# Longer rows for wo and W_down, a last product in rows of 128, and an output stored in eight rows: one change to a cached-attention decode block

## The chip, the cores and the metric

The kernel runs on one core of a Trainium2 chip. The metric is the time of one execution in device microseconds (us). Two times appear below. The time of a run is the metric; the *span* of a profile goes from the first to the last instruction of the profiled execution and is about 1.8 us shorter. Instants such as "659.29" are in us from the start of a profile's span.

## The reference, cut to what matters

Two vectors (B = 2, D = 512) go through one block of attention against a cache and one gated feed-forward block (FFN).

```python
# Hq = Hkv = 32 heads, Sk = 8192, Dh = 128, F = 1376, all bf16
h  = x + (softmax(q @ k.T * Dh**-0.5) @ v).reshape(B, 1, Hq * Dh) @ wo    # q = layernorm(x) @ wq
d  = layernorm(h)
h2 = h + (relu(d @ W_gate) * (d @ W_up)) @ W_down                         # [2, 1, 512]
```

The caches are 268 MB of the 281 MB that have to be read; wo is 4 MB, W_gate, W_up and W_down 1.4 MB each.

## The kernel before: the parts that matter here

SyncE issues all loads on one queue. K and V come in 4 MB tiles (128 partitions of 32 KB) into four slots; a step of the loop takes two heads of one batch, and every second step loads the 256 KB of wo for the four results just made. `O_cur` holds those results with the head dimension on the partitions, so wo is loaded with row `d` of each head on partition `d`: rows of 1 KB.

```python
def load_wo(dst, g, sem):
    nc.sync.dma_start(
        dst[:].rearrange("p (h n) -> p h n", n=D),
        A_wo[2*g*Dh:2*(g+1)*Dh].rearrange("(h d) n -> d h n", d=128)).then_inc(sem, 16)

def collect(T, a):                      # turns the P.V result (rows) into O_cur's layout
    nc.tensor.wait_ge(a2p, a)
    for jj in range(VJ):                # VJ = 4, float32: two passes each
        i = nc.tensor.matmul(Ob[:, 0:4], lhsT=os_sb[:, jj*Dh:(jj+1)*Dh],
                             rhs=sel[:, 4*jj:4*jj+4], start=(jj == 0), stop=(jj == VJ-1))
# ... (the loop: scores, exp, P.V, collect, o_proj with wo_cur) ...
```

At the end W_up, W_gate and W_down are loaded into a free slot. `slot[0]` holds, per partition, four rows of W_up and of W_gate, and W_down in 1 KB rows (row `r*128 + p` on partition `p`):

```python
for k, (r0, r1) in enumerate(WD_PARTS):                       # ((0, 6), (6, 10))
    nc.sync.dma_start(slot[0][:, 2*DC*F + r0*D:2*DC*F + r1*D].rearrange("p (r n) -> p r n", n=D),
        B_W_down[r0*128:r1*128].rearrange("(r p) n -> p r n", p=128)).then_inc(sem_wd[k], 16)
# ...
def ffn_in(dst, w, f0, f1):                                   # W_up, then W_gate
    for f in range(f0, f1):
        fw = 128 if f < 10 else FR                            # FR = 96, DC = 4
        for c in range(DC):
            i = nc.tensor.matmul(dst[0:fw, f*B:(f+1)*B],
                lhsT=w[:, c, f*128:f*128 + fw],               # weights: contiguous columns
                rhs=d_b[:, c*B:(c+1)*B], start=(c == 0), stop=(c == DC-1))
    return pe.run(i)
# ... hd = relu(gate) * up, in two halves ...
for k, (f0, f1) in enumerate(((0, FH), (FH, FC))):            # FH = 6, FC = 11
    pe.wait(t_hd[k], (sem_wd[k], 16))
    for f in range(f0, f1):
        for c in range(DC):                                   # result: 128 partitions x 8
            i = nc.tensor.matmul(Op[0][:, c*B:(c+1)*B], lhsT=wdn[:, f, c, :], # (wd_last for f = 10)
                                 rhs=hd[0:kp, f*B:(f+1)*B], ...)
# ... two VectorE operations add h ...
nc.sync.dma_start(out[:, 0].rearrange("b (p c) -> p b c", c=DC),              # 256 pieces of 8 bytes
                  o_c[:].rearrange("p (b c) -> p b c", b=B)).then_inc(sem_out, 16)
```

The softmax here doesn't subtract the row's maximum and nothing guards it: scores larger than these inputs give would overflow.

Of the kernel before, what the change touches and what calls it, by code (L numbers as in the profile page):

```python
# [7 lines left out]
F32 = mybir.dt.float32  # L8
BF16 = mybir.dt.bfloat16
# [30 lines left out]
def bass_sequential_preLN__gqa_block_cached__glu_gated_reglu__decode_kernel(  # L40
# [16 lines left out]
    DC = D // 128  # L57
# [13 lines left out]
    WD_PARTS = ((0, 6), (6, 10))  # L71

    with ExitStack() as es:
# [19 lines left out]
        sem_wd = [S(f"wd{i}") for i in range(3)]  # L93
# [28 lines left out]
        zr = sb("zr", [128, 4], F32)  # L122
        zi = sb("zi", [128, 4], F32)
        O_cur = sb("O_cur", [128, 4], BF16)
# [4 lines left out]
        r2 = sb("r2", [128, B], F32)  # L129
# [3 lines left out]
        o_c = sb("o_c", [128, B * DC], BF16)  # L133
# [18 lines left out]
        with nc.Block() as block:  # L152

            @block.sync
            def _(eng):
# [4 lines left out]
                def load_wo(dst, g, sem):  # L160
                    nc.sync.dma_start(
                        dst[:].rearrange("p (h n) -> p h n", n=D),
                        A_wo[2 * g * Dh:2 * (g + 1) * Dh].rearrange("(h d) n -> d h n", d=128)).then_inc(sem, 16)
# [7 lines left out]
                nc.sync.dma_start(wd_last[:], B_W_down[F - FR:]).then_inc(sem_wd[2], 16)  # L171
# [10 lines left out]
                for c in range(4):  # L182
                    pool.last()
                    pool.run(nc.gpsimd.tensor_copy(
                        out=sel[32 * c:32 * c + 32, :].rearrange("p (j q a) -> p j q a", j=VJ, q=PG),
                        in_=ident_f[32 * c:32 * c + 32, 32 * c:32 * c + 16].rearrange("p (q j a) -> p j q a", j=VJ, q=PG)))
# [163 lines left out]
                def collect(T, a):  # L350
                    nc.tensor.wait_ge(a2p, a)
                    for jj in range(VJ):
                        i = nc.tensor.matmul(  # L353
                            Ob[:, 0:4], lhsT=os_sb[:, jj * Dh:(jj + 1) * Dh],
                            rhs=sel[:, 4 * jj:4 * jj + 4], start=(jj == 0), stop=(jj == VJ - 1))
                    T.mark("ob", i)

                def z_sum(T, bank):
                    T.mark("z", nc.tensor.matmul(  # L359
                        bank[:, ZC:ZC + 8], lhsT=ones_f[:], rhs=zs[:], start=True, stop=True))  # L360

                def o_proj(T, w, b0, b1, last=False):
                    wv = w[:].rearrange("p (h n c) -> p h c n", n=128, c=DC)
                    for h in range(2):
                        for c in range(DC):
                            i = nc.tensor.matmul(
                                Wp[:, c * B + b0:c * B + b1], lhsT=wv[:, h, c, :],
                                rhs=O_cur[:].rearrange("p (b a) -> p a b", a=2)[:, h, b0:b1],
# [3 lines left out]
                with nc.Fori(0, NI, engines=OrderedEngineSet([nc.tensor.engine])):  # L372
# [7 lines left out]
                    o_proj(body, wo_cur, 0, B)  # L380
# [18 lines left out]
                o_proj(tail, wo_cur, 0, B)  # L399
# [30 lines left out]
                def normalize(bank, t_z):  # L430
                    dve.wait(t_z)
                    dve.run(nc.vector.tensor_reduce(  # L432
                        out=zr[:], in_=bank[:, ZC:ZC + 8].rearrange("p (n k) -> p n k", k=2), axis=AX.X, op=ALU.add))
# [4 lines left out]
                def o_scale(t_ob):  # L438
                    dve.wait(t_ob)
                    nc.vector.tensor_tensor(out=O_cur[:], in0=Ob[:, 0:4], in1=zi[:], op=ALU.mult).then_inc(d2p, 1)  # L440

                t_dm, t_s = {}, {}
                for p in range(NP):
# [76 lines left out]
                    elif p == NP - 2:  # L520
# [5 lines left out]
                        for k, (r0, r1) in enumerate(WD_PARTS):  # L526
                            nc.sync.dma_start(  # L527
                                slot[0][:, 2 * DC * F + r0 * D:2 * DC * F + r1 * D].rearrange("p (r n) -> p r n", n=D),
                                B_W_down[r0 * 128:r1 * 128].rearrange("(r p) n -> p r n", p=128)).then_inc(sem_wd[k], 16)
# [10 lines left out]
                o_proj(tail, wo_last, 0, B, last=True)  # L540
# [18 lines left out]
                wdn = slot[0][:, 2 * DC * F:2 * DC * F + 10 * D].rearrange("p (r n c) -> p r c n", c=DC, n=128)  # L559
                wdl = wd_last[:].rearrange("p (n c) -> p c n", c=DC)  # L560
                pe.wait(t_d)

                def ffn_in(dst, w, f0, f1):
                    for f in range(f0, f1):
                        fw = 128 if f < 10 else FR
                        for c in range(DC):
                            i = nc.tensor.matmul(
                                dst[0:fw, f * B:(f + 1) * B], lhsT=w[:, c, f * 128:f * 128 + fw],
# [3 lines left out]
                FH = 6  # L572
                pe.wait((sem_w[0], 16))
                t_u = ffn_in(Sp[1], wup, 0, FC)
                pe.wait((sem_w[1], 16))
                t_g = (ffn_in(Op[1], wgt, 0, FH), ffn_in(Wp, wgt, FH, FC))

# [79 lines left out]
```

## Time and profile before

| | before |
|---|---|
| time, median of the first three runs | 665.84 us (665.70 to 665.99) |
| bytes read, mean rate over the span | 281.05 MB, 423 GB/s |
| busy: DVE, TensorE | 70%, 51% |
| last load (W_down's second part) lands | 659.29 us |
| output issued, landed | 660.72, 663.63 us |

The first lines are from the profile's page: the span; the share of time in which the 16 DMA engines were busy, in 40 slices (tenths, 9 is 90% or more); their packets by size; and the engines' shares of the chain of waits that ended last.

```profile
span 664.0 us, 7589 instructions
...
DMA  9999999999999999999999999999999999999996
...
DMA packets 15856, 281.20 MB, mean 423 GB/s; under 512 B 1666, under 2 KB 7140, under 8 KB 7140
...
DMA 71%; DVE 26%; PE 1%; ACT 0%; issue 0%; SPq 0%; DVEq 0%
```

No slice but the last is below nine tenths. The DMA engines never rest until the last weights are in, so each nanosecond that a packet costs is a sixteenth of a nanosecond of the kernel's time. DVE's 26% of the chain is no contradiction: VectorE frees the slots, but each load is issued about 28 us before it lands.

Grouped by size, the packets' records in the trace give what a packet costs (not a view of the profile but worked out from its packet records): 8192 of 32768 B at a mean of 1220.8 ns, 256 of 11008 B at 417.0 ns, and 5474 of 1024 B at 47.8 ns.

```
packet size    before: count, mean ns     after: count, mean ns
32768 B        8192   1220.8              8192   1219.8
11008 B         256    417.0               256    418.1
 5120 B           -                        128    199.1
 4096 B           -                        128    161.9
 2048 B           -                       2048     85.2
 1024 B        5474     47.8               226     46.1
```

A line through the first two is about 10 ns per packet plus 37.8 ns per KB, and the small ones lie on it.

Next is the tail, from the timeline before. A line gives the start and the duration in us, the engine, the line of the program, the operation, what it writes and reads, how many, and in brackets how long the engine had been idle before it and what ended that.

```profile
650.93 1.06 PE L353 MATMUL Ob<-sel,os_sb 128*128 128x4 f32 x8 [0.70 <-ACT os_sb L535]
...
653.51 1.25 PEld L567 LDWEIGHTS S<-d_b,slot 128*128 128x128 bf16 x44 [0.34 <-DVE d_b L552]
...
655.96 0.72 PEld L567 LDWEIGHTS O<-d_b,slot 128*128 128x128 bf16 x24 [1.21 <-DMA slot<-in_B_W_gate_dram]
655.97 0.80 PE L567 MATMUL O<-d_b,slot 128*128 128x2 bf16 x24 [1.12 <-DMA slot<-in_B_W_gate_dram]
656.61 0.82 PEld L567 LDWEIGHTS W<-d_b,slot 128*128 128x128 bf16 x20
...
658.16 0.93 PE L611 MATMUL O<-hd,slot 128*128 128x2 bf16 x24 [0.59 <-DMA slot<-in_B_W_down_dram]
659.42 0.67 PE L611 MATMUL O<-hd,slot 128*128 128x2 bf16 x16 [0.33 <-DMA slot<-in_B_W_down_dram]
...
660.34 0.35 DVE L618 SCALAR_TENSOR_TENSOR o_c<-O,r,hb 128x4 bf16<-128x4 f32 x2 [2.35 <-PE O L611]
660.72 0.39 SPq L623 DMA_DIRECT2D out_dram<-o_c  x1
```

TensorE collects the last results (L353), multiplies W_up (the first L567), then waits 1.12 us for W_gate and 0.59 and 0.33 us for the two parts of W_down (L611). So here, too, the loads set the pace; TensorE's reserve is about 2 us in all.

### The profile page before, as it was taken

What the parts mean: (1) busy time and instruction counts of PE and PEld (TensorE: products, weight loads), DVE (VectorE), ACT (ScalarE), POOL (GpSimd) and SP (SyncE); (2) the same over time, 40 slices, a digit from 0 to 9 for tenths busy, and PEclk for the clock granted to TensorE, in tenths of its full rate; (3) what the DMA queues carried; (4) which work ended last, traced back from release to release, by engine and by line L of the source; (5) the groups of instructions that cost most, each with busy time, mean ns of one, the idle gap of its engine ahead of it and who ended that gap; (6) DMA issues with size and microseconds to landing.
All of it is one profiled execution on the core that took longest, in us unless ns stands there. A gap on an engine that the chain in (4) does not pass through costs nothing.

```text
span 664.0 us, 7589 instructions
## 1 busy us (share of the span) xinstructions
PE 339.3 (51%) x3223; PEld 220.8 (33%) x3223; DVE 465.7 (70%) x275; ACT 198.5 (30%) x416; POOL 194.1 (29%) x48
## 2 busy tenths in 40 slices
PE   2535554446545445643536545445653535554665
PEld 2413332324333223432314333222432323342444
DVE  1756887767688676787767688676678767678671
ACT  0603332223332123332213332123333213333360
POOL 2022333332233331233332133332133332134000
PEclk9999566555555665566556655665555556555657
DMA  9999999999999999999999999999999999999996
GB/s 379 413 440 424 433 438 427 430 424 428 436 438 426 420 426 438 427 435 425 430 430 428 436 418 442 423 426 436 427 434 430 428 432 426 434 427 434 428 417 239
DMA packets 15856, 281.20 MB, mean 423 GB/s; under 512 B 1666, under 2 KB 7140, under 8 KB 7140
## 3 DMA queue, kind: packets, MB, share of 16 engines
q1 hardware_dynamic: 15840, 281.06, 99.2%
q8 instruction: 5, 0.08, 0.0%
q14 instruction: 7, 0.06, 0.0%
q10 hardware_dynamic: 4, 0.00, 0.0%
HBM read 281.05 MB, written 0.00 MB: 423 GB/s over the span
## 4 chain that ended last, share of the span: by engine, by line
DMA 71%; DVE 26%; PE 1%; ACT 0%; issue 0%; SPq 0%; DVEq 0%
DMA slot<-in_A_k_cache_dram 64%; DVE prod L466 16%; DVE tb L474 7%; DMA slot<-in_B_W_down_dram 5%; DVE prod L474 3%; DMA slot<-in_A_wq_dram 2%; PE W L229 1%; ACT q_b L276 0%; PE O L271 0%; DVE q L249 0%; PE O L611 0%; SPq L523 0%; SPq L527 0%; DVE tb L262 0%; PE S L240 0%
## 5 line engine op out<-in xcount | busy, mean ns | idle before, releaser
L455 POOL COPY q2c<-q 128x8 bf16<-128x8 bf16 x32 | 190.3, 5947 | 417.2 <-DMA slot<-in_A_k_cache_dram 359.6
L466 DVE TENSOR_TENSOR prod<-slot,q_b 128x12288 bf16<-128x12288 bf16 (+1 forms) x32 | 207.7, 6492 | 130.4 <-DMA slot<-in_A_k_cache_dram 128.8
L325 PE MATMUL T<-ident_f,slot 128*128 128x128 f32 x528 | 136.5, 426 | 219.3 <-POOL q2c L455 217.0
L491 ACT ACTIVATE kT<-T 128x1024 bf16<-128x1024 bf16 x132 | 131.6, 1022 | 390.4 <-PE T L325 386.2
L325 PEld LDWEIGHTS T<-ident_f,slot 128*128 128x128 f32 x528 | 98.2, 218 | 233.4 <-POOL q2c L455 230.8
L474 DVE TENSOR_TENSOR tb<-prod 128x6144 bf16<-128x6144 bf16 (+1 forms) x64 | 136.8, 2137 | 2.2
L343 PE MATMUL O<-slot,e 128*32 128x512 bf16 x1024 | 114.7, 613 | 18.5 <-ACT e L423 18.5
L474 DVE TENSOR_TENSOR prod<-tb 128x3072 bf16<-128x3072 bf16 (+1 forms) x64 | 73.4, 1148 | 2.2
L313 PE MATMUL S<-q2c,kT 128*128 128x4 bf16 x1056 | 50.4, 170 | 37.7 <-ACT kT L491 37.7
L313 PEld LDWEIGHTS S<-q2c,kT 128*128 128x128 bf16 x1056 | 44.1, 108 | 67.8 <-ACT kT L491 65.9
L343 PEld LDWEIGHTS O<-slot,e 128*32 128x32 bf16 x1024 | 31.9, 132 | 76.2 <-issue 53.4
L353 PE MATMUL Ob<-sel,os_sb 128*128 128x4 f32 x136 | 31.0, 351 | 26.3 <-ACT os_sb L499 25.6
L353 PEld LDWEIGHTS Ob<-sel,os_sb 128*128 128x128 f32 x136 | 29.5, 320 | 28.1 <-ACT os_sb L499 26.9
L479 DVE TENSOR_REDUCE scores<-prod 128x96 f32<-128x768 bf16 (+1 forms) x32 | 30.2, 945 | 1.1
L423 ACT ACTIVATE e<-scores 64x96 bf16<-64x96 f32 (+1 forms) x64 | 19.6, 307 | 22.8 <-DVE scores L479 22.0
L432 DVE TENSOR_REDUCE zr<-Ob 128x4 f32<-128x8 f32 x15 | 2.5, 166 | 28.1 <-PE Ob L353 28.1
L423 ACT ACTIVATE e<-S 64x32 bf16<-64x32 f32 (+1 forms) x64 | 13.1, 204 | 14.9 <-PE S L313 14.5
L423 ACT ACTIVATION_READ_ACCUMULATOR e<-S 64x1 f32 x64 | 12.9, 201 | 0.7
L423 ACT ACTIVATION_READ_ACCUMULATOR e<-scores 64x1 f32 x64 | 11.8, 185 | 0.0
L359 PEld LDWEIGHTS Ob<-zs,ones_f 128*128 128x128 f32 x30 | 6.5, 269 | 11.6 <-issue 11.6
L499 ACT ACTIVATE os_sb<-O 128x512 f32<-128x512 f32 x16 | 9.6, 597 | 0.4
L276 ACT ACTIVATE q_b<-O 128x512 bf16<-128x512 f32 x8 | 4.3, 595 | 17.0 <-PE O L271 17.0
(74 smaller groups left out, 70.4 us busy)
## 6 DMA issues: line engine op xcount, KB each, us to landing
slot<-in_A_k_cache_dram SPq DMA_DIRECT2D x32, 4096.0 KB, 28.1
slot<-in_A_v_cache_dram SPq DMA_DIRECT2D x31, 4096.0 KB, 31.6
slot<-in_A_wq_dram SPq DMA_DIRECT2D x1, 4096.0 KB, 12.3
slot<-in_A_v_cache_dram SPq DMA_DIRECT2D x2, 2048.0 KB, 29.5
wo_cur<-in_A_wo_dram SPq DMA_DIRECT2D x15, 256.0 KB, 27.1
slot<-in_B_W_up_dram SPq DMA_DIRECT2D x1, 1376.0 KB, 26.7
slot<-in_B_W_gate_dram SPq DMA_DIRECT2D x1, 1376.0 KB, 29.8
slot<-in_B_W_down_dram SPq DMA_DIRECT2D x1, 768.0 KB, 31.4
```

Of the source, the lines that this page charges most:

```text
L229: i = nc.tensor.matmul(Wp[:, h * B:(h + 1) * B], lhsT=wq[:, c, h * Dh:(h + 1) * Dh], rhs=lT[:, c * B:(c + 1) * B], start=(c == 0), stop=(c ...
L313: i = nc.tensor.matmul(Sp[p % 2][:, 2 * jj:2 * jj + 4], lhsT=kv_[:, k, r, :], rhs=q2c[p % 2][:, r, :], start=(r == 0), stop=(r == 1))
L325: i = nc.tensor.transpose(Tp[g % 2][:, k * 128:(k + 1) * 128], k_t[:, j:j + 2, :].rearrange("p j d -> p (j d)").bitcast(F32), ident_f[:])
L343: i = nc.tensor.matmul(Op[0][c:c + 32, :], lhsT=e_t[q][:, j // VJ, :], rhs=v_t[:, j:j + VJ, :].rearrange("p j d -> p (j d)"), start=(q == ...
L353: i = nc.tensor.matmul(Ob[:, 0:4], lhsT=os_sb[:, jj * Dh:(jj + 1) * Dh], rhs=sel[:, 4 * jj:4 * jj + 4], start=(jj == 0), stop=(jj == VJ - 1))
L423: i = nc.scalar.activation(out=e_t[q][h, j0 // VJ:j1 // VJ, 8 * q:8 * q + 8].rearrange("p g (j a) -> p g j a", a=2)[:, :, :, a], in_=src(h ...
L455: nc.gpsimd.tensor_copy(out=q2c[p % 2][:], in_=q2[:, p]).then_inc(g2p, 1)
L466: t_dm[p] = dve.run(nc.vector.tensor_tensor(out=prod[:, 0:jd, :], in0=k_t[:, 0:jd, :], in1=qv, op=ALU.mult))
L474: dve.run(nc.vector.tensor_tensor(out=o, in0=cur[:, :, 0:half], in1=cur[:, :, half:w], op=ALU.add))
L479: t_s[p] = dve.run(nc.vector.tensor_reduce(out=sc[:, 0:jd], in_=cur, axis=AX.X, op=ALU.add))
L491: to_pe(nc.scalar.activation(out=kT[gg % 2][:], in_=Tp[gg % 2][:].bitcast(BF16), func=ACT.Copy))
L499: to_pe(nc.scalar.activation(out=os_sb[:], in_=Op[0][:], func=ACT.Copy))
```

## The change

Its intent is to make the packets fewer and the end shorter. wo comes in 2 KB rows (two rows of wo per partition), so O has to be taken out with `2*p + r` as its index: the collect becomes 16 products of 64 columns. W_down comes in rows of 5, 4 and 1 KB (ten rows per partition), so the index of `hd` on partition `p` is `10*p + f`, and W_up and W_gate are read as weights with a step of 10 columns. The last product has `hd` as the weights and W_down as the moving operand, its result lies in rows of 128, h is transposed to match, and two DMAs store four rows of 256 B each.

```diff
-    WD_PARTS = ((0, 6), (6, 10))
+    WD_PARTS = ((0, 5), (5, 9), (9, 10))
 ... load_wo
-                        dst[:].rearrange("p (h n) -> p h n", n=D),
-                        A_wo[2 * g * Dh:2 * (g + 1) * Dh].rearrange("(h d) n -> d h n", d=128)).then_inc(sem, 16)
+                        dst[:], A_wo[2 * g * Dh:2 * (g + 1) * Dh].rearrange("(p r) n -> p (r n)", r=2)).then_inc(sem, 16)
 ... collect
-                    for jj in range(VJ):
-                        i = nc.tensor.matmul(
-                            Ob[:, 0:4], lhsT=os_sb[:, jj * Dh:(jj + 1) * Dh], ...
+                    for r in range(2):
+                        for jj in range(VJ):
+                            for a_ in range(2):
+                                i = nc.tensor.matmul(
+                                    Ob[64 * a_:64 * a_ + 64, B * r:B * r + B],
+                                    lhsT=os_sb[:].rearrange("p (j d r) -> p j r d", j=VJ, r=2)[:, jj, r, :], ...
 ... W_down
-                                B_W_down[r0 * 128:r1 * 128].rearrange("(r p) n -> p r n", p=128)).then_inc(sem_wd[k], 16)
+                                B_W_down[0:10 * 128].rearrange("(p r) n -> p r n", r=10)[:, r0:r1]).then_inc(sem_wd[k], 16)
 ... ffn_in
-                                dst[0:fw, f * B:(f + 1) * B], lhsT=w[:, c, f * 128:f * 128 + fw],
+                                dst[0:fw, f * B:(f + 1) * B],
+                                lhsT=w[:, c, f:10 * 128:10] if f < 10 else w[:, c, 10 * 128:],
 ... between W_up and W_gate: h into rows
+                for k in range(4):
+                    for c in range(DC):
+                        i = nc.tensor.matmul(
+                            Tp[0][32 * k:32 * k + B, c:128:DC], lhsT=hb[:, c * B:(c + 1) * B],
+                            rhs=ident[:, 32 * k:32 * k + 32], start=True, stop=True)
 ... the last product (hd is now made in one piece)
+                    for m in range(4):
+                        i = nc.tensor.matmul(
+                            Op[0][32 * m:32 * m + B, 0:128], lhsT=hd[0:kp, f * B:(f + 1) * B],
+                            rhs=(wdn[:, f, :] if f < 10 else wd_last[:])[:, 128 * m:128 * m + 128], ...
 ... the store
-                nc.sync.dma_start(
-                    out[:, 0].rearrange("b (p c) -> p b c", c=DC),
-                    o_c[:].rearrange("p (b c) -> p b c", b=B)).then_inc(sem_out, 16)
+                for b, e in enumerate((nc.sync, nc.scalar)):
+                    e.dma_start(
+                        out[b, 0].rearrange("(k n) -> k n", n=128), o_r[b:128:32, :]).then_inc(sem_out, 16)
```

(The sums for the softmax, the variance and the sizes of the small tiles follow suit.)

More of the change, by code (lines that the diff above doesn't have):

```diff
@@ L92, in bass_sequential_preLN__gqa_block_cached__glu_gated_reglu__decode_kernel @@
         sem_w = [S(f"w{i}") for i in range(2)]
-        sem_wd = [S(f"wd{i}") for i in range(3)]
+        sem_wd = [S(f"wd{i}") for i in range(4)]
         slot = [sb(f"slot{i}", [128, SLOT], BF16) for i in range(4)]
@@ L121, in bass_sequential_preLN__gqa_block_cached__glu_gated_reglu__decode_kernel @@
         zs = sb("zs", [128, 4, 2], F32)
-        zr = sb("zr", [128, 4], F32)
-        zi = sb("zi", [128, 4], F32)
-        O_cur = sb("O_cur", [128, 4], BF16)
+        zr = sb("zr", [128, B], F32)
+        zi = sb("zi", [128, B], F32)
+        O_cur = sb("O_cur", [128, 2, B], BF16)
         hb = sb("hb", [128, DC * B], BF16)
@@ L128, in bass_sequential_preLN__gqa_block_cached__glu_gated_reglu__decode_kernel @@
         vr = sb("vr", [128, B], F32)
-        r2 = sb("r2", [128, B], F32)
+        ve = sb("ve", [128, 1], F32)
+        r2 = sb("r2", [128, 1], F32)
+        h_r = sb("h_r", [128, 128], F32)
+        o_r = sb("o_r", [128, 128], BF16)
         vh = sb("vh", [128, 2 * B], BF16)
@@ L132, in bass_sequential_preLN__gqa_block_cached__glu_gated_reglu__decode_kernel @@
         hd = sb("hd", [128, FC * B], BF16)
-        o_c = sb("o_c", [128, B * DC], BF16)
         os_sb = sb("os_sb", [128, 512], F32)
@@ L170, in _ @@
                 load_wo(wo_last, NI, sem_wl)
-                nc.sync.dma_start(wd_last[:], B_W_down[F - FR:]).then_inc(sem_wd[2], 16)
+                nc.sync.dma_start(wd_last[:], B_W_down[F - FR:]).then_inc(sem_wd[3], 16)
                 load(2, A_k_cache, 1)
@@ L184, in _ @@
                     pool.run(nc.gpsimd.tensor_copy(
-                        out=sel[32 * c:32 * c + 32, :].rearrange("p (j q a) -> p j q a", j=VJ, q=PG),
-                        in_=ident_f[32 * c:32 * c + 32, 32 * c:32 * c + 16].rearrange("p (q j a) -> p j q a", j=VJ, q=PG)))
+                        out=sel[32 * c:32 * c + 32, :].rearrange("p (j a q) -> p j a q", j=VJ, q=PG),
+                        in_=ident_f[32 * c:32 * c + 32, 32 * c:32 * c + 16].rearrange("p (q j a) -> p j a q", j=VJ, q=PG)))
                 pool.last()
@@ L351, in collect, with o_proj @@
                     nc.tensor.wait_ge(a2p, a)
-                    for jj in range(VJ):
-                        i = nc.tensor.matmul(
-                            Ob[:, 0:4], lhsT=os_sb[:, jj * Dh:(jj + 1) * Dh],
-                            rhs=sel[:, 4 * jj:4 * jj + 4], start=(jj == 0), stop=(jj == VJ - 1))
+                    for r in range(2):
[3 more added lines that the diff above has]
+                                    Ob[64 * a_:64 * a_ + 64, B * r:B * r + B],
+                                    lhsT=os_sb[:].rearrange("p (j d r) -> p j r d", j=VJ, r=2)[:, jj, r, :],
+                                    rhs=sel[:, (2 * jj + a_) * B:(2 * jj + a_) * B + B],
+                                    start=(jj == 0), stop=(jj == VJ - 1))
                     T.mark("ob", i)
                 def z_sum(T, bank):
-                    T.mark("z", nc.tensor.matmul(
-                        bank[:, ZC:ZC + 8], lhsT=ones_f[:], rhs=zs[:], start=True, stop=True))
-                def o_proj(T, w, b0, b1, last=False):
-                    wv = w[:].rearrange("p (h n c) -> p h c n", n=128, c=DC)
-                    for h in range(2):
+                    for a in range(2):
+                        i = nc.tensor.matmul(
+                            bank[64 * a:64 * a + 64, ZC:ZC + 2 * B], lhsT=ones_f[:, 0:64],
+                            rhs=zs[:].rearrange("p (b a) k -> p a b k", a=2)[:, a], start=True, stop=True)
+                    T.mark("z", i)
+                def o_proj(T, w, last=False):
+                    wv = w[:].rearrange("p (r n c) -> p r c n", n=128, c=DC)
+                    for r in range(2):
                         for c in range(DC):
                             i = nc.tensor.matmul(
-                                Wp[:, c * B + b0:c * B + b1], lhsT=wv[:, h, c, :],
-                                rhs=O_cur[:].rearrange("p (b a) -> p a b", a=2)[:, h, b0:b1],
+                                Wp[:, c * B:(c + 1) * B], lhsT=wv[:, r, c, :], rhs=O_cur[:, r, :],
                                 start=False, stop=last, skip_group_check=True)
@@ L379, in _ @@
                     nc.tensor.wait_ge(v2p, 2)
-                    o_proj(body, wo_cur, 0, B)
+                    o_proj(body, wo_cur)
                     nc.tensor.sem_inc(d2p, -1)
@@ L398, in _ @@
                 nc.tensor.wait_ge(sem_wo, 16 * NI)
-                o_proj(tail, wo_cur, 0, B)
+                o_proj(tail, wo_cur)
                 pv(tail, P0, ((j30, J, ((slot_sem[1], 256), (a2p, 5))), (0, j30, ((a2p, 7),))))
@@ L432, in normalize @@
                     dve.run(nc.vector.tensor_reduce(
-                        out=zr[:], in_=bank[:, ZC:ZC + 8].rearrange("p (n k) -> p n k", k=2), axis=AX.X, op=ALU.add))
+                        out=zr[:], in_=bank[:, ZC:ZC + 2 * B].rearrange("p (n k) -> p n k", k=2), axis=AX.X, op=ALU.add))
                     dve.last()
@@ L439, in o_scale @@
                     dve.wait(t_ob)
-                    nc.vector.tensor_tensor(out=O_cur[:], in0=Ob[:, 0:4], in1=zi[:], op=ALU.mult).then_inc(d2p, 1)
+                    nc.vector.tensor_tensor(
+                        out=O_cur[:], in0=Ob[:, 0:2 * B].rearrange("p (r b) -> p r b", b=B),
+                        in1=zi[:].unsqueeze(1).broadcast_to([128, 2, B]), op=ALU.mult).then_inc(d2p, 1)
                 t_dm, t_s = {}, {}
@@ L539, in _ @@
                 nc.tensor.wait_ge(sem_wl, 16)
-                o_proj(tail, wo_last, 0, B, last=True)
+                o_proj(tail, wo_last, last=True)
                 t = tok("om", NI)
@@ L558, in _ @@
                             for k in range(2))
-                wdn = slot[0][:, 2 * DC * F:2 * DC * F + 10 * D].rearrange("p (r n c) -> p r c n", c=DC, n=128)
-                wdl = wd_last[:].rearrange("p (n c) -> p c n", c=DC)
+                wdn = slot[0][:, 2 * DC * F:2 * DC * F + 10 * D].rearrange("p (r n) -> p r n", n=D)
                 pe.wait(t_d)
@@ L567, in ffn_in @@
                             i = nc.tensor.matmul(
-                                dst[0:fw, f * B:(f + 1) * B], lhsT=w[:, c, f * 128:f * 128 + fw],
+                                dst[0:fw, f * B:(f + 1) * B],
+                                lhsT=w[:, c, f:10 * 128:10] if f < 10 else w[:, c, 10 * 128:],
                                 rhs=d_b[:, c * B:(c + 1) * B], start=(c == 0), stop=(c == DC - 1))
                     return pe.run(i)
-                FH = 6
                 pe.wait((sem_w[0], 16))
                 t_u = ffn_in(Sp[1], wup, 0, FC)
+                for k in range(4):
[3 more added lines that the diff above has]
+                            rhs=ident[:, 32 * k:32 * k + 32], start=True, stop=True)
+                t_hr = pe.run(i)
                 pe.wait((sem_w[1], 16))
-                t_g = (ffn_in(Op[1], wgt, 0, FH), ffn_in(Wp, wgt, FH, FC))
+                t_g = ffn_in(Op[1], wgt, 0, FC)
                 dve.last()
@@ L588, in _ @@
                 dve.run(nc.vector.tensor_copy(out=u_sb[:], in_=Sp[1][:, 0:FC * B]))
+                dve.wait(t_hr)
+                dve.run(nc.vector.tensor_copy(out=h_r[:], in_=Tp[0][:, 0:128]))
                 dve.last()
-                t_hd = []
-                for k, (bank, f0, f1) in enumerate(((Op[1], 0, FH), (Wp, FH, FC))):
-                    dve.wait(t_g[k])
-                    t_hd.append(dve.run(nc.vector.scalar_tensor_tensor(
-                        out=hd[:, f0 * B:f1 * B], in0=bank[:, f0 * B:f1 * B], scalar=0.0,
-                        in1=u_sb[:, f0 * B:f1 * B], op0=ALU.max, op1=ALU.mult)))
+                dve.wait(t_g)
@@ L596, in _ @@
+                t_hd = dve.run(nc.vector.scalar_tensor_tensor(
+                    out=hd[:], in0=Op[1][:, 0:FC * B], scalar=0.0,
+                    in1=u_sb[:], op0=ALU.max, op1=ALU.mult))
                 pe.wait(t_vh)
-                for k in range(2):
-                    i = nc.tensor.matmul(Sp[0][:, 64:64 + B], lhsT=onesn[:], rhs=vh[:, k * B:(k + 1) * B],
-                                         start=(k == 0), stop=(k == 1))
+                for m in range(4):
+                    for k in range(2):
+                        i = nc.tensor.matmul(Sp[0][32 * m:32 * m + B, 32:33], lhsT=vh[:, k * B:(k + 1) * B],
+                                             rhs=onesn[:, 0:1], start=(k == 0), stop=(k == 1))
@@ L600, in _ @@
                 t_var = pe.run(i)
                 dve.wait(t_var)
-                dve.run(nc.vector.tensor_scalar_add(out=vr[:], in0=Sp[0][:, 64:64 + B], scalar1=eps))
+                dve.run(nc.vector.tensor_scalar_add(out=ve[:], in0=Sp[0][:, 32:33], scalar1=eps))
                 dve.last()
-                dve.run(nc.vector.reciprocal(out=r2[:], in_=vr[:]))
-                pe.wait((sem_wd[2], 16))
-                for k, (f0, f1) in enumerate(((0, FH), (FH, FC))):
-                    pe.wait(t_hd[k], (sem_wd[k], 16))
-                    for f in range(f0, f1):
-                        kp = 128 if f < 10 else FR
-                        for c in range(DC):
-                            i = nc.tensor.matmul(
-                                Op[0][:, c * B:(c + 1) * B], lhsT=wdn[:, f, c, :] if f < 10 else wdl[:, c, :], rhs=hd[0:kp, f * B:(f + 1) * B],
-                                start=(f == 0 and c == 0), stop=(f == FC - 1), skip_group_check=True)
+                dve.run(nc.vector.reciprocal(out=r2[:], in_=ve[:]))
@@ new lines, in _ @@
+                pe.wait((sem_wd[3], 16), t_hd)
+                order = [(10, 3)] + [(f, k) for k, (f0, f1) in enumerate(WD_PARTS) for f in range(f0, f1)]
+                for n, (f, k) in enumerate(order):
+                    pe.wait((sem_wd[k], 16))
+                    kp = 128 if f < 10 else FR
+                    for m in range(4):
+                        i = nc.tensor.matmul(
+                            Op[0][32 * m:32 * m + B, 0:128], lhsT=hd[0:kp, f * B:(f + 1) * B],
+                            rhs=(wdn[:, f, :] if f < 10 else wd_last[:])[:, 128 * m:128 * m + 128],
+                            start=(n == 0), stop=(n == FC - 1))
@@ L616, in _ @@
                 dve.wait(t_y)
-                for b in range(B):
-                    t = dve.run(nc.vector.scalar_tensor_tensor(
-                        out=o_c[:, b * DC:(b + 1) * DC],
-                        in0=Op[0][:, 0:DC * B].rearrange("p (c b) -> p b c", b=B)[:, b, :], scalar=r2[:, b:b + 1],
-                        in1=hb[:].rearrange("p (c b) -> p b c", b=B)[:, b, :], op0=ALU.mult, op1=ALU.add))
-                sp.wait(t)
-                nc.sync.dma_start(
-                    out[:, 0].rearrange("b (p c) -> p b c", c=DC),
-                    o_c[:].rearrange("p (b c) -> p b c", b=B)).then_inc(sem_out, 16)
-                nc.sync.wait_ge(sem_out, 16)
+                t = dve.run(nc.vector.scalar_tensor_tensor(
+                    out=o_r[:], in0=Op[0][:, 0:128], scalar=r2[:, 0:1], in1=h_r[:], op0=ALU.mult, op1=ALU.add))
+                sp.wait(t)
+                act.wait(t)
+                for b, e in enumerate((nc.sync, nc.scalar)):
+                    e.dma_start(
+                        out[b, 0].rearrange("(k n) -> k n", n=128), o_r[b:128:32, :]).then_inc(sem_out, 16)
+                nc.sync.wait_ge(sem_out, 16 * B)
     return nc
```

## The prediction

> **What bounds the kernel now.** The DMA engines. The page's slices show DMA at 9 tenths throughout; stretches of 10 us between 500 and 650 us show a DMA share of 0.98 to 1.03 at 419 to 439 GB/s. The chain of waits is 71% DMA; PE is busy 51% and DVE 70% of the span, and every load is issued about 28 us before it lands, so the queue never runs dry. The time is therefore the sum of the packets' times, plus a tail after the last landing. The packet records: 8192 packets of 32 KB at 1221 ns, 256 of 11 KB at 417 ns, 5474 of 1 KB at 47.8 ns. That is a line, about 10 ns per packet plus 37.8 ns per KB.
>
> The tail (timeline): W_down's last part lands at 659.29 us; 20 matmuls 0.8 us, two DVE operations 0.35 us, output issued at 660.72 and landed 2.9 us later, end 664.0.
>
> **Stream.** wo: 16 loads of 256 packets of 1 KB become 128 of 2 KB (estimate 86 ns from the line): per load 0.765 to 0.69 us on each of 16 engines, 1.2 us in all. W_down: 1280 packets become 384 of 5, 4 and 1 KB: 3.8 to 3.3 us, 0.55 us. The stream ends about 1.8 us earlier. All of that is on the critical path, since DMA has no gap.
>
> **Loop.** The collecting product grows from 8 to 32 fp32 passes with 64 columns. Eight took 1.87 us at half clock; I estimate 3.5 us. PE has slack in the loop: nothing lost there.
>
> **Tail, saved.** After the last landing 4 matmuls of 128 columns instead of 20 and one DVE operation instead of two: about 0.6 us. Output in 8 rows of 256 B instead of 256 pieces of 8 B: I guess 0.5 us of the 2.9. The Trainium skill ("DMA: Bandwidth & Descriptors", Specifications) puts the minimum for line rate at 512 B; both forms lie below it, and no run yet shows the difference.
>
> **Tail, added on PE.** Before, PE waited 1.1 us for W_gate after finishing with W_up. Now: the last collect at full clock takes about 2.0 instead of 1.06 us (+0.9); transposing h, 16 small matmuls, +0.5; the 44 W_down matmuls all come after one hd, about 30 ns each, because four column groups overlap (P·V's 512-column matmuls came every 112 ns at half clock, a quarter of their streaming time). And W_up and W_gate are now read as weights with a column stride of 10 elements. Weight loads came every 25 to 27 ns with stride 1 or 2 and every 33.4 ns with stride 4. The Trainium skill ("SBUF — State Buffer", on cachelines) says that an access crossing into a new 16-byte line pays; at 20 bytes every column does. I estimate 33 to 67 ns each over 88 loads: 0.5 to 3.5 us more. So the tail turns from waiting for W_down to waiting for PE, and eats part of the gain.
>
> **Sum.** DMA-bound it would be about 2.9 us less (663.0); with the PE tail at 50 ns per load, about 1 us less. I predict 664.6 us, 8 in 10 between 663.0 and 667.0. Faster by over 2%: 0.01; within 2%: 0.98; slower: 0.01.
>
> **What would show it.** Packets: no 1 KB ones for wo, 2 KB ones near 86 ns; the last weight packet near 657.5 us on the span's clock instead of 659. Weight loads at the FFN line more than 33 ns apart. Little or no wait of the last product's matmuls for W_down. Output landing near 2.4 us.
>
> **What would make it wrong.** W_down's rows staying 1 KB descriptors; stride-10 loads costing nothing (663) or over 70 ns (667 and up); column groups not overlapping (107 ns each, +3 us); PE at half clock in the last collect (+1.5 us).

## The result

Ratios in this document are the mean time of one kernel's fast runs over that of the other's of the same rounds, so they are not quite the ratio of the medians quoted beside them.

| | before | after |
|---|---|---|
| first set: median (range), 4 runs each | 665.91 (665.70 to 666.10) | 665.20 (664.59 to 666.01) us |
| ratio, 95% interval | | 0.999 (0.9973 to 1.0007) |
| second set: median, 9 and 5 runs | 665.73 | 664.85 (664.65 to 665.01) us |
| ratio, 95% interval | | 0.9986 (0.9972 to 0.9999) |
| last W_down part lands | 659.29 | 657.52 us |
| output issued | 660.72 | 660.48 us |
| end of the profile's span | 664.0 | 662.8 us |

The loads end 1.77 us earlier, the output is issued only 0.24 us earlier. The page's lines of after:

```profile
span 662.8 us, 8513 instructions
...
DMA  9999999999999999999999999999999999999995
...
DMA packets 12673, 281.22 MB, mean 424 GB/s; under 512 B 1426, under 2 KB 1652, under 8 KB 3956
...
DMA 66%; DVE 28%; PE 4%; ACT 1%; issue 0%; DVEq 0%
```

There are 3183 packets fewer, and TensorE's share of the chain went from 1% to 4%. The tail of after, in the same form:

```profile
649.61 1.13 PE L356 MATMUL Ob<-sel,os_sb 128*64 128x2 f32 x32 [0.70 <-ACT os_sb L544]
...
652.27 2.73 PEld L575 LDWEIGHTS S<-d_b,slot 128*128 128x128 bf16 x44 [0.34 <-DVE d_b L561]
...
655.02 0.41 PE L586 MATMUL T<-ident,hb 128*2 128x32 bf16 x16
...
655.36 2.73 PEld L575 LDWEIGHTS O<-d_b,slot 128*128 128x128 bf16 x44
...
658.62 0.28 PE L627 MATMUL O<-wd_last,hd 96*2 96x128 bf16 x4 [0.30 <-DVE ve L618]
...
658.68 1.28 PE L627 MATMUL O<-slot,hd 128*2 128x128 bf16 x40
660.10 0.35 DVE L634 SCALAR_TENSOR_TENSOR o_r<-O,r,h_r 128x128 bf16<-128x128 f32 x1 [1.35 <-PE O L627]
660.48 0.65 SPq L639 DMA_DIRECT2D out_dram<-o_r  x1
```

Compare the brackets: no product waits for a weight load from memory any more. W_gate landed at 654.37 and W_down at 657.52, but TensorE came to W_gate at 655.36 and to W_down at 658.62. The two groups of 44 weight loads (L575) take 2.73 us each; before, the same work (L567) took 1.25 and 1.54 us (0.72 + 0.82, the second group being in two pieces). From one weight load's start to the next, the median is 58 ns in after and 26 ns in before. The clock is not the reason: in after the granted clock was 1.00 from 652.3 to 653.6 and 0.50 from 653.8 on, and both groups have the same median of 58 ns. The tail has changed its master, from the DMA engines to TensorE.

One load still sets where this chain begins, in both kernels: the last weight loads of P·V wait for the V cache (0.33 us before, until 649.18; 0.27 us after, until 647.81). That is how the shorter stream still reaches the end: the collect starts 1.32 us earlier (649.61 for 650.93). But from there to the issue of the output it takes 10.87 us instead of 9.79, and so 0.24 us are left.

### The profile page after: what moved, and what is told of

Same layout as the page of the kernel before. It is cut to its first block, busy times and chain, and to the rows that moved or that the text cites. A ratio compares the mean times of both kernels' runs of the same rounds, so it can differ in the third digit from the quotient of the medians.

```text
span 662.8 us, 8513 instructions
## 1 busy us (share of the span) xinstructions
PE 338.6 (51%) x3685; PEld 220.4 (33%) x3685; DVE 465.5 (70%) x274; ACT 198.3 (30%) x416; POOL 194.1 (29%) x48
## 4 chain that ended last, share of the span: by engine, by line
DMA 66%; DVE 28%; PE 4%; ACT 1%; issue 0%; DVEq 0%
DMA slot<-in_A_k_cache_dram 64%; DVE prod L475 16%; DVE tb L483 8%; DVE prod L483 3%; DMA slot<-in_A_wq_dram 2%; PE T L326 1%; PE O L344 1%; PE W L230 1%; ACT q_b L277 0%; PE S L575 0%; PE O L575 0%; PE O L272 0%; ACT kT L500 0%; PE S L314 0%; PE O L627 0%
## 5 line engine op out<-in xcount | busy, mean ns | idle before, releaser
L356 PE MATMUL Ob<-sel,os_sb 128*64 128x2 f32 x544 | 31.1, 245 | 26.2 <-ACT os_sb L508 25.5
L356 PEld LDWEIGHTS Ob<-sel,os_sb 128*64 128x64 f32 x544 | 29.7, 217 | 28.1 <-ACT os_sb L508 26.9
L439 DVE TENSOR_REDUCE zr<-Ob 128x2 f32<-128x4 f32 x15 | 2.4, 162 | 28.3 <-PE Ob L356 28.3
```

The costliest lines, as they stand in the source:

```text
L356: i = nc.tensor.matmul(Ob[64 * a_:64 * a_ + 64, B * r:B * r + B], lhsT=os_sb[:].rearrange("p (j d r) -> p j r d", j=VJ, r=2)[:, jj, r, :], ...
```

## The experiments

Twelve runs were made in three calls; each call shares its runs of the kernel before, so differences are taken within a call. "−2.5" means us below the median of before in the same call.

One warning on the correctness check. The FFN's contribution to h2 is so small beside h that the check doesn't notice a wrong one: e1_stride1 below multiplies W_down's rows with the wrong elements of hd and still counts as correct. That the changed kernel, b_wdown5, e3 and e4 compute the right thing rests on their indices alone.

### First call: is it the stride?

Theory A: the strided weight loads made TensorE the limit of the tail. Rival B: the tail's other additions did (collect in 32 passes, transposing h, 44 wide products). Rival C: the stream's gain is itself uncertain.

**after_again**: no edit.

> The changed kernel once more, unaltered, as the yardstick for the three kernels beside it. Its four runs so far lie in two groups, 664.6 to 664.7 and 665.7 to 666.0 us, where the kernel before stays within 0.4 us. Theory A (the tail now hangs on TensorE: a gapless chain from the last P.V product to the output): the groups come back and are a matter of the granted clock in the tail, so a profile of a slow one shows the same DMA landings and longer TensorE pieces between 645 and 660 us. Rival C (the gain of the stream is itself uncertain from run to run): a slow profile shows the last landing of W_down later than 657.5 us by about 1 us. Time 664.6 to 666.0, ratio to before about 0.999.

Measured: 664.85 us (664.65 to 665.01), −0.88. The profile has the same 58 ns loads and W_down landing at 657.54. The slow group of the first set (665.69 and 666.01) did not come back and no profile of it exists, so its cause stays open. The two landings of W_down in hand differ by 0.02 us, which is against C but doesn't exclude it: e1_stride1 below has the same loads and landed W_down at 657.97, 0.45 us later, and its P·V waited for V until 648.28 instead of 647.81. So the stream does vary by about half a microsecond from run to run. The mean granted clock over the span was not lower in the two slow runs (0.626 and 0.615) than in the two fast ones (0.586 and 0.581); the clock in their tails is not known.

**e1_stride1**: contiguous weights, wrong result.

```diff
-                                lhsT=w[:, c, f:10 * 128:10] if f < 10 else w[:, c, 10 * 128:],
+                                lhsT=w[:, c, f * 128:f * 128 + fw],
```

> The changed kernel with W_up and W_gate read as weights in contiguous columns again; W_down's rows then no longer match, so the result is wrong on purpose. Theory A: the two groups of 44 weight loads fall from 2.73 us to about 1.2 us each (27 ns a load instead of 62), TensorE waits for W_down again, the last product ends about 0.45 us after W_down's last landing at 657.5, the output is issued near 658.4 and the time is 662.3 to 663.0 us, 2 us or more below the changed kernel in the same rounds. Rival B (the other additions to the tail, the 32-pass collect, the transposes of h and the 44 wide matmuls, use up the gain): less than 0.5 us below the changed kernel.

Measured: 662.70 us (662.60 to 663.03), −3.03, ratio 0.9953 (0.9939 to 0.9966). The timeline of e1_stride1:

```profile
652.69 1.43 PEld L575 LDWEIGHTS S<-d_b,slot 128*128 128x128 bf16 x44 [0.34 <-DVE d_b L561]
...
654.93 1.47 PEld L575 LDWEIGHTS O<-d_b,slot 128*128 128x128 bf16 x44 [0.56 <-DMA slot<-in_B_W_gate_dram]
...
657.69 0.41 PEld L627 LDWEIGHTS O<-slot,hd 128*2 128x2 bf16 x20 [0.25 <-DMA slot<-in_B_W_down_dram]
658.54 0.35 DVE L634 SCALAR_TENSOR_TENSOR o_r<-O,r,h_r 128x128 bf16<-128x128 f32 x1 [1.49 <-PE O L627]
```

The loads take half as long, TensorE waits for W_gate and W_down again, and the time falls by 2.15 us against the changed kernel in the same call. Theory A holds. The output was issued at 658.92 and not near 658.4, because W_down landed at 657.97. B falls: its additions are all still in this kernel. They cost less than the waits they fill.

**e2_wdown_1kb**: W_down as before, in 1 KB rows (and so contiguous weights); all the rest as changed.

```diff
-  lhsT=w[:, c, f:10 * 128:10] if f < 10 else w[:, c, 10 * 128:],
+  lhsT=w[:, c, f * 128:f * 128 + fw],
-  B_W_down[0:10 * 128].rearrange("(p r) n -> p r n", r=10)[:, r0:r1]).then_inc(sem_wd[k], 16)
+  B_W_down[r0 * 128:r1 * 128].rearrange("(r p) n -> p r n", p=128)).then_inc(sem_wd[k], 16)
```

> The changed kernel with W_down loaded as before, in 1 KB rows, and so with contiguous columns of W_up and W_gate; the result is right. It undoes W_down's layout alone. Theory A: the stream ends about 0.55 us later than in the changed kernel (1280 packets of 48 ns in place of 384), but TensorE's tail is 3 us shorter, so the time is bound by W_down's landing again: 662.8 to 663.6 us, better than the changed kernel by 1.5 to 2 us. Then the 5 KB rows of W_down are a loss as a whole. Rival B: about 0.5 us slower than the changed kernel.

Measured: 663.17 us (662.96 to 663.54), −2.56, ratio 0.996 (0.9946 to 0.9973). So W_down's long rows, with the stride they bring, cost the changed kernel 1.68 us (664.85 − 663.17). In this profile W_down landed at 657.99, and the last product ran from 657.45 to 658.79; the lower clock in the last collect (below) had a hand in that.

**e3_rows2**: W_down in 2 KB rows, in groups of 256 rows (row `256*g + 2*p + r` on partition `p`), so that the weights' step is 2 columns.

```diff
-    WD_PARTS = ((0, 5), (5, 9), (9, 10))
+    WD_PARTS = ((0, 4), (4, 8), (8, 10))
-  slot[0][:, ...].rearrange("p (r n) -> p r n", n=D),
-  B_W_down[0:10 * 128].rearrange("(p r) n -> p r n", r=10)[:, r0:r1]).then_inc(sem_wd[k], 16)
+  slot[0][:, ...].rearrange("p (g m) -> p g m", m=2 * D),
+  B_W_down[r0 * 128:r1 * 128].rearrange("(g p r) n -> p g (r n)", p=128, r=2)).then_inc(sem_wd[k], 16)
-  lhsT=w[:, c, f:10 * 128:10] if f < 10 else w[:, c, 10 * 128:],
+  lhsT=w[:, c, f // 2 * 256 + f % 2:f // 2 * 256 + 256:2] if f < 10 else w[:, c, 10 * 128:],
```

> The changed kernel with W_down in 2 KB rows (two rows of it per partition in five groups of 256), so that W_up and W_gate are read with a column stride of 2; the result is right. Theory A: weight loads every 27 ns as with stride 2 in the score products, W_down's 640 packets of about 86 ns cost 0.17 us more than 384, last landing near 657.7, time 662.5 to 663.3 us: better than both kernels. Rival B: as the changed kernel within 0.5 us.

Measured: 663.15 us (662.65 to 663.60), −2.58, ratio 0.9958 (0.9945 to 0.9972). The median step from load to load is 27 ns. The kernel beats both. Its profile, however, shows a tail without waits again: the last product ran without a stop from 657.54 to 658.88, while W_down landed at 658.10. The main reason is the clock of TensorE. In the first two lines are the last P·V products and collect of e3_rows2 (timeline), in the third the last collect of e2_wdown_1kb:

```profile
647.50 2.85 PE L344 MATMUL O<-slot,e 128*32 128x512 bf16 x32
...
651.06 1.13 PE L356 MATMUL Ob<-sel,os_sb 128*64 128x2 f32 x32 [0.71 <-ACT os_sb L544]
```

```profile
650.22 1.87 PE L356 MATMUL Ob<-sel,os_sb 128*64 128x2 f32 x32 [0.69 <-ACT os_sb L544]
```

In after the P·V products took 1.91 us and the collect 1.13. Here the stretches' granted clock was 0.65 for the 2.85 us and 0.50 for the 1.87 us, against 1.00 for both in after. In e2_wdown_1kb it had been 1.00 from 645 to 648 and was 0.50 from 649 on. Of the 1.45 us by which e3's collect started later than after's, the slower P·V products are 0.94; the rest is their later start (647.50 for 646.99). So the moment at which the clock rises and falls near the end, which differs from run to run, is worth up to about 1 us once the tail hangs on TensorE. That fits the two groups of after's first four runs and the spread of e3's five; it isn't shown for them.

### Second call: each part by itself

**b_wo**: the kernel before with the wo part alone (load, collect, sums, scaling, as in the diff above; the edit also moved the declaration of the output tile `o_c`).

> The kernel before with the wo part of the change alone: wo in 2 KB rows, the collect in 16 products of 64 columns, the sums and the scaling to match; W_down, the last product and the store as before. The tail then waits for W_down's landing as before, so what the stream saves should all be seen. Theory A: 2048 packets of 85 ns in place of 4096 of 48 ns on 16 engines, 1.3 us less; W_down lands near 658.0 instead of 659.29, time 664.2 to 664.8 us against 665.7. Rival (the larger collect delays the loop or the tail): 665.3 us or more.

Measured: 665.48 us (665.32 to 666.00), −0.45, ratio 0.9996 (0.9982 to 1.0009). By its time that is the rival's case, but not for its reason: neither the loop nor the tail was delayed. W_down did land 1.32 us earlier (657.97) and the output was issued 1.32 us earlier (659.40), yet it landed at 663.35, 3.95 us after its issue instead of 2.91.

**b_out_rows**: the kernel before, with a tile of zeros stored in the new form, wrong result.

```diff
-                nc.sync.dma_start(out[:, 0].rearrange("b (p c) -> p b c", c=DC),
-                    o_c[:].rearrange("p (b c) -> p b c", b=B)).then_inc(sem_out, 16)
+                for b, e in enumerate((nc.sync, nc.scalar)):           # o_r: zeros
+                    e.dma_start(out[b, 0].rearrange("(k n) -> k n", n=128), o_r[b:128:32, :]).then_inc(sem_out, 16)
```

> The kernel before, computing all as before, but what is stored at the end, after the same wait, is a tile of zeros in eight rows of 256 B by two DMAs; the result is wrong on purpose. It measures the store's form alone. From issue to the end of the span was 3.3 us before and 2.3 us after the change. If the pieces' size makes it, the time is 0.9 to 1.1 us below before, 664.6 to 664.9 us; if the difference came from something else in the changed tail, it is within 0.3 us of before.

Measured: 664.87 us (664.72 to 664.90), −1.06, ratio 0.9985 (0.9972 to 0.9999). The store's form alone is worth 1.06 us: 1.92 us from issue to landing. "Form" is three things here, the size of the pieces, their number and the split over two issuing engines, and no run separates them.

**b_wdown5**: the kernel before with W_down alone in rows of 6 and 4 KB (the text says 3 to 5, a slip) and the stride of 10.

```diff
-  B_W_down[r0 * 128:r1 * 128].rearrange("(r p) n -> p r n", p=128)).then_inc(sem_wd[k], 16)
+  B_W_down[0:10 * 128].rearrange("(p r) n -> p r n", r=10)[:, r0:r1]).then_inc(sem_wd[k], 16)
-  lhsT=w[:, c, f * 128:f * 128 + fw],
+  lhsT=w[:, c, f:10 * 128:10] if f < 10 else w[:, c, 10 * 128:],
```

> The kernel before with W_down alone in rows of 3 to 5 KB (two loads of six and four rows per partition), so that W_up and W_gate are read with a column stride of 10; the last product and the store as before, the result right. Theory A: W_down lands about 0.55 us earlier, but W_up's and W_gate's weight loads take 2.7 us each instead of 1.3 and 1.5; TensorE's wait of 1.1 us for W_gate and of 0.9 us for W_down absorb most of it, the last product ends near 660.7 to 661.0 instead of 660.2, and the time is 666.1 to 666.6 us: this part alone is a loss. Rival (W_down's longer rows help by themselves): 665.2 us or less.

Measured: 666.16 us (665.92 to 666.67), +0.23, ratio 1.0004 (0.999 to 1.0018), at the lower edge of what A expected; the interval includes no change. The loads are 58 ns apart here too, and the output was issued at 661.43 instead of 660.72. W_down landed at 659.02, 0.27 us earlier and not 0.55. The part is no gain; most of its cost falls into waits that the kernel before had. In its timeline the last product no longer waits for W_down:

```profile
653.95 2.75 PEld L567 LDWEIGHTS S<-d_b,slot 128*128 128x128 bf16 x44 [0.35 <-DVE d_b L552]
...
659.34 1.46 PE L611 MATMUL O<-hd,slot 128*128 128x2 bf16 x40
...
661.43 0.40 SPq L623 DMA_DIRECT2D out_dram<-o_c  x1
```

**e4_hr_late**: e3_rows2 with the transposing of h moved behind W_gate's products.

```diff
                 t_u = ffn_in(Sp[1], wup, 0, FC)
-                ... 16 products into Tp[0]; t_hr = pe.run(i) ...
                 pe.wait((sem_w[1], 16))
                 t_g = ffn_in(Op[1], wgt, 0, FC)
 ...            t_var = pe.run(i)
+                ... the same 16 products; the copy into h_r follows r2 ...
```

> The changed kernel with W_down in 2 KB rows and stride 2 (as the third kernel of the first set, 663.15 us), and with the 16 products that transpose h moved from before W_gate's products to after them, into the wait for hd. In that kernel's profile TensorE had a gapless chain again (the last product began 657.5 and ended 658.9, W_down having landed at 658.1), so 0.3 us less work ahead of it should show in part: 662.6 to 663.2 us. If W_down's landing is the limit, no difference from 663.15.

Measured: 662.87 us (662.81 to 663.14), −3.06, ratio 0.9956 (0.9942 to 0.997): the lowest time of a kernel that is right, though its interval overlaps those of e2 and e3. The timeline of e4_hr_late shows both waits back, and the transposing in a gap:

```profile
654.61 1.54 PE L575 MATMUL O<-d_b,slot 128*128 128x2 bf16 x44 [0.89 <-DMA slot<-in_B_W_gate_dram]
...
656.14 0.40 PE L610 MATMUL T<-ident,hb 128*2 128x32 bf16 x16
...
657.81 0.10 PEld L626 LDWEIGHTS O<-slot,hd 128*2 128x2 bf16 x8 [0.33 <-DMA slot<-in_B_W_down_dram]
...
658.33 0.35 DVE L633 SCALAR_TENSOR_TENSOR o_r<-O,r,h_r 128x128 bf16<-128x128 f32 x1 [1.40 <-PE O L626]
658.71 0.65 SPq L638 DMA_DIRECT2D out_dram<-o_r  x1
```

e3 and e4 ran in different calls, and this profile had the clock up at the right time, so how much the move itself gave isn't settled: 0.48 us by the differences to before, 0.28 by the medians themselves, 0.13 by the ratios.

### Third call: where did b_wo's gain go?

Theory D: the store in 8-byte pieces swallowed it.

**b_wo_rows**: b_wo with the store of b_out_rows (zeros, wrong).

> The wo part alone (as b_wo) with the store of b_out_rows: a tile of zeros in eight rows of 256 B, wrong result on purpose. In b_wo the stream did end 1.3 us earlier and the output was issued 1.3 us earlier (659.40 for 660.72), but its landing took 3.95 us from the issue in place of 2.91, and only 0.45 us were left. Theory D: the store in 8-byte pieces swallowed the rest, and in rows the whole shows: 1.3 + 1.0 us, 663.4 to 663.8. Rival (something other than the store's form holds the end back): 664.4 us or more.

Measured: 663.61 us (663.56 to 663.85), −2.31, ratio 0.9964 (0.9951 to 0.9978). With the store in rows the wo part is worth 1.25 us (2.31 − 1.06), as the packets say. D holds.

**e4_out8**: e4 with zeros stored in 256 pieces of 8 bytes, wrong.

> The best kernel so far (stride 2, late transposes of h, 662.87 us) with its store replaced by a tile of zeros in 256 pieces of 8 bytes, as the kernel before stores; wrong result on purpose. Theory D: from issue to landing 2.9 to 4 us in place of 1.92, so 663.9 to 665.0 us. If the landing is 2.9 us after the issue, the 3.95 of b_wo was peculiar to that program; if near 4, an early store in pieces is held up in general.

Measured: 663.91 us (663.78 to 664.13), −2.01, ratio 0.9969 (0.9956 to 0.9983). The store took 2.9 us: an early store in pieces isn't held up in general; 3.95 us belong to b_wo.

**b_wo_again** and **before_again**: no edits.

> The wo part alone once more, unaltered, for a second profile of its store. Theory D: the store lands 3.5 us or more after its issue again and the time is within 0.3 us of 665.48. If it lands 2.9 us after, as in the kernel before, the time is near 664.5 and the first set was chance.

> The kernel before, unaltered, for a second profile of its store: 2.91 us from issue to landing in the first. A second one between 2.8 and 3.1 says that 2.9 is steady for this program; 3.5 or more says that the landing of 8-byte pieces is loose by about 1 us and that a single profile of it can't be leaned on. Time 665.5 to 666.1.

Measured: b_wo_again 665.85 us (665.70 to 666.24), −0.07, ratio 0.9998 (0.9983 to 1.0013); before_again 665.88 us in its one run. The store's landing came as Theory D said; the time of b_wo_again lies 0.37 us from 665.48, just outside the 0.3 that it allowed. Here are SyncE's waits for the landing of the output, one line each from the waits of before, b_wo, b_wo_again, e4_out8 and after (us in total, times, longest; the wait begins when the issue ends):

```profile
SPq L152 <- DMA out_dram<-o_c: 2.5, 1, 2.5
```

```profile
SPq L152 <- DMA out_dram<-o_c: 3.6, 1, 3.6
```

```profile
SPq L152 <- DMA out_dram<-o_c: 3.6, 1, 3.6
```

```profile
SPq L155 <- DMA out_dram<-o_c: 2.5, 1, 2.5
```

```profile
SPq L154 <- DMA out_dram<-o_r: 1.3, 1, 1.3
```

The store in pieces took 2.91 and 2.96 us from issue to landing in two profiles of before, 3.95 in both of b_wo, 3.05 in b_wdown5 and 2.90 in e4_out8. In all of them the packets started 0.90 to 0.91 us after the issue and the 256 of them ended within 0.24 us of the first one's start; the difference lies between packet and landing, which were 1.76 to 2.81 us apart. In rows it took 1.92 to 1.93 us in all eight profiles: the packets started later, 1.23 to 1.25 us after the issue, but the landing followed the last of them within 0.32 to 0.34 us. Why b_wo's pieces land a microsecond later than those of the other programs is open: the tile is declared at another place than in before, but in e4_out8 too, and no run varied its place alone.

### The account

Laying the runs in a row, each with its difference to before in its own call:

| kernel | difference | step |
|---|---|---|
| before, stored in rows (b_out_rows) | −1.06 | store: −1.06 |
| and wo in 2 KB rows (b_wo_rows) | −2.31 | wo: −1.25 |
| and the last product in rows (e2_wdown_1kb) | −2.56 | product: −0.25 |
| and W_down in 5, 4 and 1 KB rows: the change (after_again) | −0.88 | W_down: +1.68 |
| W_down in 2 KB rows in its place (e3_rows2) | −2.58 | −1.70 against the change |
| and h transposed later (e4_hr_late) | −3.06 | |

The steps combine three calls, with intervals of about ±0.9 us on each difference (0.13% of the time), so the product's 0.25 is not distinguishable from nothing. The other three terms each have a profile behind them.

## Why the prediction was right

It forecast 664.6 us, 663.0 to 667.0, and "within 2%" with 0.98. The medians are 665.2 and 664.85. Its mechanism was right, but that the number came so close is partly luck. Two terms were mis-sized to the same side, both too pessimistic: the output (0.5 us) and the collect (0.8 us). Against them stand loads that took 58 ns and not 50, and a saving of 0.6 us after the last landing that didn't show. The prediction doesn't say how it came from its terms to "about 1 us less", so how exactly they cancel can't be told.

- **Stream: right.** It forecast 86 ns for a 2 KB packet and a stream that ends 1.8 us earlier; measured were 85.2 ns and 1.77 us (659.29 to 657.52). W_down's rows did become 5, 4 and 1 KB packets, but their share is smaller than the 0.55 us forecast: from W_gate's landing to W_down's it took 3.37 to 3.51 us in the seven profiles with 1 KB rows and 3.08 to 3.15 in the four with long rows, about 0.3 us less. The sum of packet times overstates it.
- **The tail turns to TensorE: right.** "The tail turns from waiting for W_down to waiting for PE, and eats part of the gain": all waits for weights vanish from after's tail, and e1_stride1 shows that the stride is what did it.
- **Stride-10 loads: right within its range.** It said 33 to 67 ns each and reckoned with 50; measured were 58. Over 88 loads that is 2.7 us more than before (mean step 59 against 28 ns) where it had 0.5 to 3.5. Its ground was the Trainium skill, "SBUF — State Buffer", in "Door 1: The DMA port swizzle": an access that crosses into a new 16-byte line pays. The runs agree: 58 ns at a step of 20 bytes, 25 to 27 at 2 and 4 bytes. They show that the step costs; that the crossing of lines is the reason they don't show, as no run has a step of 5 to 9 columns or of more than 10.
- **The output: the term that was mis-sized.** The step "I guess 0.5 us of the 2.9" measured 1.06 us by the clock of runs (b_out_rows) and 0.99 by the landing (2.91 to 1.92).
- **The collect: mis-sized too, as a cost that hardly came.** "About 2.0 instead of 1.06 us (+0.9)" in the tail measured 1.13 (+0.07), and in the loop 1.88 instead of the 3.5 forecast, against 1.87 before. Twice the columns in all, four times the passes, the same time: its weight loads started in pairs 7 ns apart (median step 7, mean 29 ns) where the full-width ones came every 111. That a pair is the two halves side by side is a reading; the profile doesn't tell the passes apart. The prediction had foreseen overlap of column groups for W_down's 44 products (1.37 us measured from the first weight load on, its 30 ns each) but hadn't applied it here.
- **Fewer VectorE operations: no gain.** One operation of 128 columns takes 0.35 us; the two small ones together took 0.35. And the saving of "4 matmuls instead of 20" after the last landing couldn't show, as TensorE got there 1.1 us after the landing.
- **Half clock in the last collect: real as a risk.** It happened in e2_wdown_1kb (1.87 instead of 1.13 us), 0.74 where the prediction said 1.5.

## What to carry to other kernels

A layout that saves time on the DMA side is paid for by whoever reads it: here ten rows per partition saved about 0.3 us by the landings and cost 2.7 us of strided weight loads, and two rows per partition saved about 0.2 us (3.20 to 3.23 us from W_gate's landing to W_down's in three profiles) at no cost in weight loads. The sums of packet times put the two savings at 0.57 and 0.41 us (1280 packets of 47.8 ns come to 3.82 us on 16 engines, 640 of 85.2 to 3.41, 128 each of 199.1, 161.9 and 46.1 to 3.26). When the DMA engines are the limit, look at how much waiting the other engines have left in the tail before spending on them; once that is gone, what the last loads gain (here W_down's) doesn't reach the end. And measure a store to its landing, not to its issue: 2 KB in 256 pieces landed 1 to 2 us later than in 8 rows, and hid about 1 us of a gain of 1.3 us in one program.

## What the Trainium skill lacked or had wrong

- "SBUF — State Buffer", "Door 1: The DMA port swizzle", says that two hits per 16-byte line suffice for full bandwidth and puts the free step at 8 elements of bf16. For weight loads of 128 columns the runs show 25 ns per load at full granted clock and 27 at half at a step of 1 or 2 elements, 33 ns at 4 (two hits per line), and 58 ns at 10, at either clock: a step of 4 isn't quite free, and no page gives the size of the penalty.
- "TensorE: Matmul & The Clock Gate", "Part 3: Packing small matmuls — row/col tiling", says that weight loads overlap with matmuls in flight only when the row group differs. For products that differ in the column half it gives no time of a weight load. In the collect all 128 rows are used and only the column half differs, and weight loads of about 138 ns start 7 ns apart in pairs; 32 passes of 64 columns take 1.13 us, 8 of 128 columns 1.06. This shows loads beside loads; as the ends of matmuls are modelled in the profile, it doesn't prove the sentence wrong.
- "DMA: Bandwidth & Descriptors" gives a fixed cost of about 2.0 us for a DMA issued from GpSimd and says that pieces under 512 B cost more, but not how much for a store of 2 KB. Stores from SyncE and ScalarE show 1.92 us from issue to landing for eight rows of 256 B, and 2.9 to 3.95 us for 256 pieces of 8 bytes, with nothing in the packets' own times (15 to 21 and 9 ns) that would make up the difference. The stores in rows were also two DMAs instead of one.
- The same page, "Bandwidth", gives about 10.5 ns per packet as the floor of a 4 KB load issued from GpSimd. That is the time of one transfer divided by its packets, not the time of a packet on its engine, whose measured time against its size the page doesn't give. On a saturated queue of SyncE the runs show, on one of the 16 engines, about 10 ns per packet plus 37.8 ns per KB, from 1 KB (47.8 ns) to 32 KB (1221 ns).
